# Splitting the first MLP weights differently between two loads, and adding a partial sum one chunk later, in a decode block on one core

## The chip, the cores and the metric

The kernel runs on one core of a Trainium2 chip. The metric is the time on the device of one execution, in microseconds (us); lower is better. Five engines of the core work side by side, each through its own queue of instructions: TensorE (PE, with its weight loads shown as PEld), VectorE (DVE), ScalarE (ACT), GpSimd (POOL) and SyncE (SP), which issues nearly all transfers.

## What is computed

The reference is a transformer block for one new token in each of four sequences: attention over a cache, then an MLP.

```python
B, Sq, D = 4, 1, 448          # attention: 16 query heads, 8 cached heads of 256
W = 1024                      # the last 1024 of 4096 cached positions
q = (layernorm(x) @ wq).reshape(B, Sq, 16, 256)
scores = einsum("bhqd,bhkd->bhqk", q, k) * 256 ** -0.5
o = einsum("bhqk,bhkd->bhqd", softmax(scores), v)
h = x + o.reshape(B, Sq, 4096) @ wo

y = layernorm(layernorm(h))   # the block's layernorm and the MLP's own
u = gelu(y @ w1 + b1)         # w1: 448 x 1792
h2 = h + u @ w2 + b2          # w2: 1792 x 448
```

All arrays are float32.

## The kernel before

The work goes head by head over the eight cached heads. Keys, values and projection weights are laid out on the host so that they come in large transfers, each into a slot of a ring of three (`t0`, `ta`, `tb`, `tc`, `td`, and at the end `te0` to `te2`). The order of TensorE's, SyncE's and ScalarE's instructions is the order of the source; VectorE's and GpSimd's is chosen when the kernel is built. All loads are issued by SyncE on one queue and land one behind the other. The last three slots take, in this order: the last head's keys (`te0`), the values and output weights of head 6 (`te1`), the values of head 7 in three pieces (`te2`), its output weights, then w1 in two pieces (`te0`), and w2 in four pieces of 8, 3, 2 and 1 chunks of 448 columns (`te2`).

The change is in the MLP at the end. There a small number of rows (four sequences) meets large weights, so the output columns are split into four quadrants, which stand on the partitions 0 to 31, 32 to 63, 64 to 95 and 96 to 127. `FQ` is 448, a quarter of the 1792 hidden columns.

- **Statistics.** `h` is the sum behind the attention. `d` and `z` are `h` with its mean taken off, once and twice. ScalarE squares both and sums along the row (`dv`, `zv`). `row_mean` (line 390) folds the four quadrants' sums into one by a matmul with the matrix `fold`. `rsqrt` (lines 145 and 146) adds the epsilon on VectorE and raises to the power of -1/2 on GpSimd. `r1` and then `s`, a product of both roots, come of it.
- **First product.** `z` is transposed to `zT`, in four chunks of 128 features; the last chunk has 64. For each chunk `a`, four matmuls (`j`, one for each quadrant of the hidden columns) add to `pu` (line 429). The weights come from `w1t`, a list of four column ranges of the slot `te0`: three of 1792 columns, and a small one of 896 columns, into whose two halves of the partitions the last 64 features are packed. `w1_part` picks the rows and columns for `a` and `j`. Since the scale `s` belongs to the row, it is applied behind the product: line 442 computes `pu * s + b1` in two column ranges, line 443 the GELU, lines 448 and 450 transpose, and lines 452 and 455 write `gT`.
- **Second product.** The hidden features are 14 chunks (`NFC`). Chunks 0 to 7 go into `pa`, each chunk with one matmul of 448 columns into one of four quadrants (line 462); ScalarE copies `pa` to `pas` (line 466). Chunks 8 to 13 go into `py` with four matmuls each (line 472), one for each quadrant of the output columns. `add_quadrants` (line 253) adds the four quadrants of `pas` into `py` with the matrix `sel`. Line 478 adds `h` and the bias and line 479 writes the output.

`keep_warm` puts matmuls on zeros into waits. A float32 matmul of the source shows as two in the profile, so a chunk of four matmuls is eight in it.

Of the kernel before, what the change touches and what calls it, by code (L numbers as in the profile page):

```python
# [11 lines left out]
ALU = mybir.AluOpType  # L12
# [7 lines left out]
F = 1792  # L20
P = 128
H = P // 2
ND = 4
NKC = W // P
NFC = F // P
FQ = F // 4
Q = 32
CACHE = NKC * B * DH
# [7 lines left out]
def block_kernel(ctx: ExitStack, tc, rows, wq0, k0, wq1, la, lb, lc, ld, k7, vo, w1, w2, out):  # L36
    nc = tc.nc
# [12 lines left out]
    def slot(name):  # L50
        return ring.tile([P, SLOT], F32, tag="r", name=name)

    def load(t, at, src, pieces=None):
        dst = t[:, at : at + src.shape[-1]]
        at = 0
        for n in pieces or (src.shape[-1],):
            nc.sync.dma_start(dst[:, at : at + n], src[:, at : at + n])  # L57
            at += n
        return dst

    def cut(t, sizes):
        parts, at = [], 0
        for n in sizes:
            parts.append(t[:, at : at + n])
            at += n
        return parts
# [18 lines left out]
    def output_weights(t):  # L85
        return t.rearrange("p (j e) -> p j e", j=4)
# [18 lines left out]
    zT = const.tile([P, ND, Q], F32, name="zT")  # L105
# [37 lines left out]
    def rsqrt(dst, var, name):  # L143
        ve = work.tile(list(dst.shape), F32, tag="ve", name=f"ve_{name}")
        nc.vector.tensor_scalar_add(ve, var, EPS)  # L145
        nc.gpsimd.tensor_tensor(dst, ve, mhalf[: dst.shape[0], : dst.shape[1]], op=ALU.pow)  # L146
# [78 lines left out]
    def columns(t, j):  # L225
        if j < 3:
            return t[:, j * P : (j + 1) * P].rearrange("p (i c) -> p i c", i=2)
        return t[:, None, 3 * P :].to_broadcast([t.shape[0], 2, H])
# [22 lines left out]
    def add_quadrants(dst, t, start):  # L251
        for j in range(4):
            nc.tensor.matmul(dst[j * Q : (j + 1) * Q], sel, columns(t, j), start=start, stop=False)
# [76 lines left out]
    e = [slot(f"te{i}") for i in range(3)]  # L330
# [2 lines left out]
    vt, wot = chunks(v), output_weights(wot)  # L333
    vt_last = chunks(load(e[2], 0, vo[1][:, :CACHE], (CACHE // 4, CACHE // 2, CACHE // 4)))
    wo_last = output_weights(load(e[1], CACHE + WEIGHTS, vo[1][:, CACHE:]))
    w1t = cut(load(e[0], CACHE, w1, (2 * F, F + F // 2)), (F, F, F, F // 2))
    w2t = cut(load(e[2], CACHE, w2, (8 * D, 3 * D, 2 * D, D)), NFC * (D,))
    p, rec_last = softmax(g + 1, scores(g + 1, kt))

# [34 lines left out]
    for i in range(4):  # L374
        for j in range(4):
            nc.tensor.matmul(
                ph[j * Q : (j + 1) * Q], oT[(g + 1) % 2][:, i, :], columns(wo_last[:, i, :], j),
                start=False, stop=(i == 3),
# [2 lines left out]

    def w1_part(a, j):
        if a < 3:
            return slice(0, P), w1t[a][:, FQ * j : FQ * (j + 1)]
        rows = slice(H * (j // 2), H * (j // 2) + H)
        return rows, w1t[a][rows, FQ * (j % 2) : FQ * (j % 2 + 1)]


    def row_mean(sums, at, name):
        nc.tensor.matmul(at, fold, sums, start=True, stop=True)  # L390
        return at

    def stat(name):
        return once.tile([P, 1], F32, tag=name, name=name)
# [3 lines left out]
    hs, ds, dv, zv = (stat(n) for n in ("hs", "ds", "dv", "zv"))  # L398
    nc.vector.scalar_tensor_tensor(h, last, 1.0, xb, op0=ALU.mult, op1=ALU.add, accum_out=hs)
    pm = ps_m.tile([P, 2], F32, tag="m", name="pm")  # L400
    m = row_mean(hs, pm[:, 0:1], "m")
# [4 lines left out]
    m = row_mean(ds, pm2[:, 0:1], "m2")  # L406
# [13 lines left out]
    r1 = stat("r1")  # L420
    s = stat("r2")
    u = once.tile([P, FQ], F32, tag="u", name="u")
    pu = ps_s.tile([P, 512], F32, tag="s", name="pu")[:, :FQ]
    pv = ps_m.tile([P, 2], F32, tag="m", name="pv")
    for a in range(ND):
        m = Q if a == 0 else B
        for j in range(4):
            rows, w = w1_part(a, j)
            nc.tensor.matmul(
                pu[j * Q : j * Q + m, :], zT[rows, a, :m], w, start=(a == 0), stop=(a == ND - 1),  # L430
            )
        if a == 0:
            rsqrt(r1, row_mean(dv, pv[:, 0:1], "v1"), "r1")
        if a == 1:
            v2 = stat("v2")
            nc.vector.tensor_scalar(v2, row_mean(zv, pv[:, 1:2], "v2"), r1, r1, op0=ALU.mult, op1=ALU.mult)
            rsqrt(s, v2, "r2")
            nc.vector.tensor_mul(s, s, r1)


    for cols in (slice(0, 2 * P), slice(2 * P, FQ)):
# [16 lines left out]
    first = 8  # L458
    pa = ps_w.tile([P, D], F32, tag="acc", name="pa")
    for c in range(first):  # L460
        j, m = c % 4, Q if c < 4 else B
# [6 lines left out]
    for c in range(first, NFC):  # L468
        for j in range(4):
            m, n = (Q, 2) if c == first else (B, 2 if j < 3 else 1)  # L470
            w = columns(w2t[c], j) if n == 2 else w2t[c][:, None, 3 * P :]
            nc.tensor.matmul(  # L472
                py[j * Q : j * Q + m, :n, :], gT[:, c, :m], w, start=(c == first), stop=(c == NFC - 1),
            )
        if c == first + 1:
            add_quadrants(py, pas, False)
    res = once.tile([P, P], F32, tag="res", name="res")
    nc.vector.tensor_add(res, py.rearrange("p i c -> p (i c)"), hb)
# [72 lines left out]
```

## Time and profile before

| | |
|---|---|
| median of three runs | 214.09 us (214.06 to 214.11) |
| the profiled execution's own time | 214.17 us |
| its span, first to last instruction | 212.4 us |
| TensorE's mean granted clock | 0.847 of full speed |
| busy share of the span: PE, DVE, ACT, POOL | 65%, 18%, 10%, 3% |
| moved by transfers | 88.46 MB, mean 417 GB/s |

The profile is of one execution. The busy share of an engine is that over the whole span; the end of the kernel, where the change lies, has to be read from the timeline and from the chain of work that ended last. In rows of instructions the first number is the start in us from the span's start, the second the duration; `out<-in` names the tiles; square brackets hold the idle time ahead of the instruction and what ended it.

### The profile page before, as it was taken

The page shows a single profiled execution, that of the slowest core. Times are in us where ns is not written, and L with a number is a line of the kernel's source. Part 1 is how long each engine was busy: PE and PEld are TensorE (multiplying, and loading weights), DVE is VectorE, ACT ScalarE, POOL GpSimd, SP SyncE. Part 2 cuts the span into 40 slices and gives each one's busy share as a digit, 9 for nine tenths or more (in the row PEclk, how much of TensorE's full clock was granted, in tenths as well). Part 3 has the DMA queues.
Part 4 walks back from the last instruction along what each step waited for, and adds up shares of the span by engine and source line. Part 5 has one row for each costly group of instructions (what it writes and reads, how often), then busy time and mean ns, then how long its engine had stood idle before and what let it go on. Part 6 is the DMA issues. An engine that isn't in the chain of part 4 may idle for free.

```text
span 212.4 us, 2289 instructions
## 1 busy us (share of the span) xinstructions
PE 138.0 (65%) x965; PEld 47.7 (22%) x965; DVE 38.4 (18%) x167; ACT 21.2 (10%) x52; POOL 5.6 (3%) x17
## 2 busy tenths in 40 slices
PE   0457825862970595189398189238908879997884
PEld 0322211220220221023123022113202322323332
DVE  1420220320230012012214013100301223123220
ACT  2010210110020100012003001101000301010311
POOL 6100000000000000000000000000000000000100
PEclk9999995797698579769859959955965899999999
DMA  7999898989999999989999999998989989999991
GB/s 284 440 388 534 361 488 371 470 374 509 408 395 517 407 407 396 479 382 477 385 477 446 422 407 481 419 442 383 490 349 466 441 384 428 426 407 427 430 400 66
DMA packets 3457, 88.46 MB, mean 417 GB/s; under 512 B 412, under 2 KB 692, under 8 KB 1272
## 3 DMA queue, kind: packets, MB, share of 16 engines
q1 hardware_dynamic: 3392, 88.29, 97.0%
q8 instruction: 7, 0.11, 0.2%
q10 hardware_dynamic: 56, 0.05, 0.1%
q14 instruction: 2, 0.02, 0.0%
HBM read 88.26 MB, written 0.07 MB: 416 GB/s over the span
## 4 chain that ended last, share of the span: by engine, by line
DMA 77%; PE 17%; SPq 2%; DVE 1%; ACT 1%; issue 1%; ACTq 0%
DMA tb<-lb 23%; DMA ta<-la 21%; DMA td<-ld 20%; DMA te<-w 13%; PE s L172 7%; PE po L216 4%; SPq L57 2%; PE pq L152 1%; PE ppt L204 1%; PE acc L245 1%; PE pa L462 1%; SPq L265 1%; PE pqt L158 1%; ACT qs L154 1%; PE py L472 0%
## 5 line engine op out<-in xcount | busy, mean ns | idle before, releaser
L177 DVE TENSOR_REDUCE mx<-s 128x1 f32<-128x512 f32 x16 | 11.1, 691 | 60.5 <-PE s L172 60.5
L172 PE MATMUL s<-ta,qT 128*32 128x512 f32 x64 | 12.7, 966 | 8.1 <-DMA ta<-la 8.1
L154 ACT COPY qs<-pq 128x512 f32<-128x512 f32 x8 | 4.7, 586 | 116.9 <-PE pq L152 116.9
L188 ACT ACTIVATE p<-s,nm 128x512 f32<-128x512 f32 x16 | 10.9, 687 | 46.2 <-DVE nm L184 46.2
L172 PE MATMUL s<-td,qT 128*32 128x512 f32 x32 | 7.3, 1061 | 12.2 <-DMA td<-ld 12.2
L233 DVE TENSOR_SCALAR o<-po,rec 128x512 f32<-128x512 f32 x8 | 6.0, 751 | 46.3 <-PE po L216 46.3
L216 PE MATMUL po<-tb,pT 128*32 128x512 f32 x32 | 7.3, 1061 | 10.6 <-DMA tb<-lb 10.6
L152 PE MATMUL pq<-tc,yT 128*32 128x512 f32 (+1 forms) x20 | 3.9, 891 | 14.7 <-DMA tc<-lc 14.7
L204 PE MATMUL ppt<-ident,p 128*128 128x128 f32 x64 | 10.5, 286 | 0.7 <-ACT p L188 0.4
L216 PE MATMUL po<-tc,pT 128*32 128x512 f32 x64 | 10.6, 823 | 0.0
L158 PE MATMUL pqt<-ident,qs 128*128 128x128 f32 x32 | 6.6, 341 | 6.0 <-ACT qs L154 6.0
L172 PE MATMUL s<-tb,qT 128*32 128x512 f32 x64 | 9.2, 724 | 0.0
L204 PEld LDWEIGHTS ppt<-ident,p 128*128 128x128 f32 x64 | 6.7, 140 | 6.3 <-ACT p L188 6.3
L160 DVE TENSOR_REDUCE sm<-pqt 128x16 f32<-128x64 f32 x8 | 1.8, 224 | 33.7 <-PE pqt L158 33.7
L216 PE MATMUL po<-te,pT 128*32 128x512 f32 x64 | 7.5, 597 | 0.4 <-DMA te<-vo 0.3
L172 PE MATMUL s<-t,qT 128*32 128x512 f32 x32 | 6.2, 953 | 1.9 <-DMA t<-k 1.9
L216 PE MATMUL po<-td,pT 128*32 128x512 f32 x64 | 7.3, 595 | 0.0
L158 PEld LDWEIGHTS pqt<-ident,qs 128*128 128x128 f32 x32 | 4.2, 169 | 12.0 <-ACT qs L154 10.3
L172 PEld LDWEIGHTS s<-ta,qT 128*32 128x32 f32 x64 | 3.0, 168 | 16.8 <-issue 13.9
L237 PE MATMUL pot<-ident,o 128*128 128x128 f32 x32 | 5.3, 287 | 2.2 <-DVE o L233 2.2
L146 POOL TENSOR_TENSOR r<-ve_r,mhalf 128x1 f32<-128x1 f32 x2 | 1.1, 542 | 190.7 <-DVE ve_r L145 190.7
L208 DVE COPY pT<-ppt 128x16 f32<-128x16 f32 x32 | 4.7, 171 | 7.6 <-PE ppt L204 7.6
(131 smaller groups left out, 114.2 us busy)
## 6 DMA issues: line engine op xcount, KB each, us to landing
tc<-lc SPq DMA_DIRECT2D x2, 7936.0 KB
td<-ld SPq DMA_DIRECT2D x2, 7936.0 KB
ta<-la SPq DMA_DIRECT2D x2, 7040.0 KB
tb<-lb SPq DMA_DIRECT2D x2, 7040.0 KB
te<-vo SPq DMA_DIRECT2D x1, 4992.0 KB
t<-k SPq DMA_DIRECT2D x1, 4864.0 KB
te<-k SPq DMA_DIRECT2D x1, 4096.0 KB
te<-w SPq DMA_DIRECT2D x2, 1792.0 KB
```

What stands on the lines that cost most here:

```text
L57: nc.sync.dma_start(dst[:, at : at + n], src[:, at : at + n])
L152: nc.tensor.matmul(pq[j * Q : (j + 1) * Q, cols], y, w, start=True, stop=True)
L154: nc.scalar.copy(qs, pq)
L158: nc.tensor.transpose(pt[:, i, :], qs[:, i * P : (i + 1) * P], ident)
L172: nc.tensor.matmul(s[b * Q : (b + 1) * Q, :], qT[g % 2][:, c, b, :], kt[:, c, b, :], start=(c == 0), stop=(c == 1),)
L177: nc.vector.reduce_max(m, s, axis=AX.X)
L188: nc.scalar.activation(p[:, h * 512 : (h + 1) * 512], halves[h], AF.Exp, bias=nm, scale=SCALE, accum_out=sums[:, h : h + 1],)
L204: nc.tensor.transpose(pt[:, c, :], p[:, (4 * h + c) * P : (4 * h + c + 1) * P], ident)
L208: nc.vector.tensor_copy(pT[g % 2][:, 2 * h : 2 * h + 2, :, i * REP : (i + 1) * REP], src[:, :, i, :, :REP])
L216: nc.tensor.matmul(po[b * Q : (b + 1) * Q], pT[g % 2][:, c, b, :], vt[c][:, :, b, :], start=(c == 0), stop=(c == NKC // 2 - 1),)
L233: nc.vector.tensor_scalar_mul(o, po, rec)
L237: nc.tensor.transpose(pt[:, i, c], o[:, i, c * P : (c + 1) * P], ident)
```

## The change

w1 is still loaded in two pieces, but the pieces are cut at another place. Before, the first held chunks 0 and 1 and the second chunk 2 and the small chunk. Now the small chunk stands behind chunk 1 in the slot and in the host's array, so that the first piece holds chunks 0, 1 and the small one, and the second only chunk 2. The products are made in that order (0, 1, small, 2). The two folds of the statistics and the work on `r1` and `s` behind them stand ahead of all four chunks; before, they stood behind chunk 0 and chunk 1. In the second product, `pas` is added behind chunk 10 in place of chunk 9.

```diff
-    w1t = cut(load(e[0], CACHE, w1, (2 * F, F + F // 2)), (F, F, F, F // 2))
+    w1t = cut(load(e[0], CACHE, w1, (2 * F + F // 2, F)), (F, F, F // 2, F))
...
         if a < 3:
-            return slice(0, P), w1t[a][:, FQ * j : FQ * (j + 1)]
+            return slice(0, P), w1t[3 if a == 2 else a][:, FQ * j : FQ * (j + 1)]
         rows = slice(H * (j // 2), H * (j // 2) + H)
-        return rows, w1t[a][rows, FQ * (j % 2) : FQ * (j % 2 + 1)]
+        return rows, w1t[2][rows, FQ * (j % 2) : FQ * (j % 2 + 1)]
...
-    for a in range(ND):
+    rsqrt(r1, row_mean(dv, pv[:, 0:1], "v1"), "r1")
+    v2 = stat("v2")
+    nc.vector.tensor_scalar(v2, row_mean(zv, pv[:, 1:2], "v2"), r1, r1, op0=ALU.mult, op1=ALU.mult)
+    rsqrt(s, v2, "r2")
+    nc.vector.tensor_mul(s, s, r1)
+    for a in (0, 1, 3, 2):
         m = Q if a == 0 else B
         for j in range(4):
             rows, w = w1_part(a, j)
             nc.tensor.matmul(
-                pu[j * Q : j * Q + m, :], zT[rows, a, :m], w, start=(a == 0), stop=(a == ND - 1),
+                pu[j * Q : j * Q + m, :], zT[rows, a, :m], w, start=(a == 0), stop=(a == 2),
             )
-        if a == 0:
-            rsqrt(r1, row_mean(dv, pv[:, 0:1], "v1"), "r1")
-        if a == 1:
-            v2 = stat("v2")
-            nc.vector.tensor_scalar(v2, row_mean(zv, pv[:, 1:2], "v2"), r1, r1, op0=ALU.mult, op1=ALU.mult)
-            rsqrt(s, v2, "r2")
-            nc.vector.tensor_mul(s, s, r1)
...
-        if c == first + 1:
+        if c == first + 2:
             add_quadrants(py, pas, False)
...
     w1 = packed(np.asarray(B_w1))
+    w1 = np.concatenate([w1[:, : 2 * F], w1[:, 3 * F :], w1[:, 2 * F : 3 * F]], axis=1)
```

## The prediction

> **What bounds the kernel now.** I read the page first, for where the time goes as a whole.
>
> ```profile
> span 212.4 us, 2289 instructions
> ...
> DMA 77%; PE 17%; SPq 2%; DVE 1%; ACT 1%; issue 1%; ACTq 0%
> ```
>
> The chain that ended last is three quarters transfer. The change touches only the last eleven microseconds, so the share says little; what counts is which wait ends last there. Next, therefore, the end of that chain in order of time (start, length, what it was).
>
> ```profile
> 177.69 28.09 DMA te<-w
> 205.78 0.14 issue
> 205.92 1.75 PE pa L462 x16
> ...
> 207.74 0.54 ACT pas L466
> ...
> 209.69 0.29 DVE res L478
> ```
>
> The chain does not pass through the first MLP product, its scaling or the GELU at all. It runs through one transfer into a `te` slot, landed at 205.78 (the 8·D piece of w2, since the partial product `pa` is released by it), then `pa`, the copy `pas`, the last products and the output. So there are two places to judge: does anything ahead of 205.78 matter, and what can be gained behind it. The third view is the timeline, engine by engine, for the stretch ahead of 205.78. Columns: start, duration, engine, line, operation.
>
> ```profile
> 198.10 0.39 PE L345 MATMUL warm<-idle 128*32 128x512 bf16 x1
> 198.44 0.96 PE L429 MATMUL pu<-te,zT 128*32 128x448 f32 x8
> 199.33 0.38 PE L390 MATMUL pv<-dv,fold 128*128 128x1 f32 x2
> 199.64 0.93 PE L429 MATMUL pu<-te,zT 128*4 128x448 f32 x8
> 200.50 0.38 PE L390 MATMUL pv<-zv,fold 128*128 128x1 f32 x2
> 201.31 1.80 PE L429 MATMUL pu<-te,zT 128*4 128x448 f32 x16 [0.42 <-DMA te<-w]
> ```
>
> ```profile
> 199.75 0.16 DVE L145 TENSOR_SCALAR ve_r<-pv 128x1 f32<-128x1 f32 x1 [1.36 <-PE pv L390]
> 201.00 0.28 DVE L436 TENSOR_SCALAR v<-pv,r 128x1 f32<-128x1 f32 x1 [1.09 <-PE pv L390]
> 201.31 0.15 DVE L145 TENSOR_SCALAR ve_r<-v 128x1 f32<-128x1 f32 x1
> 202.12 0.16 DVE L438 TENSOR_TENSOR r<-r,r 128x1 f32<-128x1 f32 x1 [0.66 <-POOL r L146]
> 203.25 0.81 DVE L442 SCALAR_TENSOR_TENSOR u<-pu,r,rs 128x256 f32<-128x256 f32 x2 [0.97 <-PE pu L429]
> 205.35 0.21 DVE L452 COPY gT<-put 128x48 f32<-128x48 f32 x1 [1.29 <-PE put L450]
> ```
>
> The 16 matmuls from 201.31 are chunks 2 and 3 of the first MLP product, released by the second load of w1. They end at 201.31 + 1.80 = 203.11, DVE's scaling follows at 203.25, and `gT` is written at 205.35 + 0.21 = 205.56. `pa` could have gone then; its weights landed 0.22 us later. The chain of the first product thus has 0.22 us to spare.
>
> **The change, part 1: w1's split and its order.** Removed: TensorE's wait of 0.42 us ahead of 201.31, for everything but chunk 2. Added: 448 KB in the first load, and that load's landing is now later. The size of the second load, and when the two landings let TensorE go, stand in the issues and in the instructions of lines 429 and 390:
>
> ```profile
> te<-w SPq DMA_DIRECT2D x1, 1344.0 KB
> ```
>
> ```profile
> L429 PEldq EVENT_SEMAPHORE  x1: 51/51/51, 198.0 to 198.0; - x1
> ```
>
> ```profile
> L390 PEldq EVENT_SEMAPHORE  x1: 51/51/51, 199.9 to 199.9; - x1
> ```
>
> The first load let TensorE go at 198.0, the second at 201.31. In these 3.3 us 1344 KB landed, so 448 KB more in the first take 3.3 / 3 = 1.1 us: it lands at 199.1, and the second, behind the same bytes in the same queue, still at 201.3. Nothing is added to the queue in bytes, transfers or order, so the w2 pieces stay at their times, 205.78 among them.
>
> With the products held to 199.1, the two sums go first. The fold of `dv` can follow the warm matmul: 198.10 + 0.39 = 198.49. Its reader on DVE starts 0.42 after it (199.33 to 199.75) and takes 0.16, to 199.07. The fold of `zv` writes the same small tile: in the row above its semaphore wait stands at 199.9, when that DVE reader is done (199.75 + 0.16), so it now starts at 199.1. A product follows a fold by 0.31 (199.33 to 199.64): the first is at 199.42, and the load of 199.1 is no wait. Queued behind this new wait for DVE on TensorE are all sixteen product groups; this 0.3 us is counted in the 199.42.
>
> Four chunks then run without a break: 0.96 for the first, and for each further one at most 1.80 - 0.93 = 0.87, which is what the second of two chunks added at 201.31 with its change from whole to half rows. The end is 199.42 + 0.96 + 3 x 0.87 = 202.99, against 203.11: 0.12 us earlier. If the wait for DVE costs nothing, 0.3 us more. Chunk 2, now last, starts at 202.99 - 0.93 = 202.06, behind its load's 201.31, so no wait takes the old one's place. The scale `s` was ready at 202.12 + 0.16 = 202.28, 1.78 after its fold at 200.50; it comes at 199.1 + 1.78 = 200.9, two microseconds before DVE needs it.
>
> So `gT` is ready at 205.1 to 205.45 instead of 205.56. The cover over this gain is the landing at 205.78, and it is complete: part 1 is worth **0 us**. Both ends: up to 0.14 gained (the step "issue" ahead of `pa`, if some of it is `gT` and not the transfer); a loss only if the chain slips by 0.12 + 0.22 = 0.34 us against my sum. I take 0, as the chain's own row names the transfer.
>
> **Part 2: `pas` folded in behind chunk 10.** Here nothing is hidden by w2's first piece.
>
> ```profile
> 207.42 0.64 PE L472 MATMUL py<-te,gT 128*32 128x128 f32 x16
> 208.32 0.43 PE L253 MATMUL py<-pas,sel 128*32 128x128 f32 x8 [0.27 <-ACT pas L466]
> 208.57 1.05 PE L472 MATMUL py<-te,gT 128*4 128x128 f32 x32
> ```
>
> Chunks 8 and 9 are the 16 matmuls at 207.42. TensorE is then idle until `pas` is copied (207.74 + 0.54 = 208.28), and the eight matmuls with `sel` start at 208.32. Chunks 10 to 13 are the last 32, in 1.05. The length of one is in the group's row (ns: least, median, most):
>
> ```profile
> L472 PE MATMUL py<-te,gT x48: 219/272/273, 207.4 to 209.3; 128*4 128x128 f32 x30, 128*4 128x64 f32 x10, 128*32 128x128 f32 x8
> ```
>
> The last one's 0.27 is its way through the array, so one chunk takes (1.05 - 0.27) / 4 = 0.20 to issue. Chunk 10 is in the same piece of w2 as 8 and 9, so it needs nothing new, and its 0.20 goes into the idle 0.27. Put ahead of `sel`, it delays `sel` by nothing: 207.42 + 0.64 + 0.20 = 208.26, before 208.28. If that cover were gone (`pas` ready earlier), chunk 10 would cost its 0.20 there again, and the sum would be zero.
>
> Behind `sel` there are then three chunks, 0.20 us less. What is late next is w2's last piece, needed by chunk 13 alone. Its landing stands in no row; the two stretches around its end bound it:
>
> ```profile
> 208.20:208.40 0.20, 0.08 (x4) 0.08 (x8) 0.00 (x0) 0.07 (x1) 0.00 (x0) 1.00 0.35 134
> 208.40:208.60 0.20, 0.20 (x12) 0.20 (x16) 0.00 (x0) 0.00 (x0) 0.00 (x0) 1.00 0.01 0
> ```
>
> The last columns are the busy share of the transfer engines and GB/s: the stream's last bytes move at about 208.4. Chunk 13 started at 208.57 + 3 x 0.20 = 209.17, in one run with the others, so its weights were there; it now can at 208.57 + 2 x 0.20 = 208.97. The landing lies between 208.4 and 209.17: at the early end the gain is 0.20 us, at the late end 0. I take **0.15 us**, nearer the early end, since from 208.4 on nothing moves and 208.97 is 0.5 us behind that.
>
> The sum: 0 + 0.15. The profiled execution took 214.17 us (span 212.4 and 1.8 around it), so 214.02; it stands 0.08 above the median of 214.09, which gives **213.94 us**. A measurement of this kernel can tell about 0.2%, 0.43 us, from no change, so I forecast no difference. The forecast's own range is 213.75 to 214.10.
>
> **The rivals.** The rate of the stream by stretches:
>
> ```profile
> 190.00:195.00 5.00, 4.05 (x47) 1.59 (x43) 1.10 (x3) 0.00 (x0) 0.00 (x0) 1.00 1.05 443
> 201.00:204.00 3.00, 2.55 (x19) 0.42 (x19) 1.34 (x5) 0.24 (x1) 0.54 (x1) 1.00 0.98 410
> 204.00:206.00 2.00, 1.47 (x15) 1.15 (x19) 0.26 (x2) 0.77 (x4) 0.00 (x0) 1.00 0.95 387
> 206.00:208.00 2.00, 2.00 (x32) 0.76 (x31) 0.00 (x0) 0.26 (x1) 0.00 (x0) 1.00 0.82 322
> ```
>
> *Faster: w2 lands sooner.* The stream ran at 443 GB/s in 190 to 195, but at 410 and 387 in 201 to 206. If that was TensorE's work beside it, and the new order takes it away, the 3 x 410 + 2 x 387 = 2004 KB would pass in 4.5 us instead of 5: 0.48 gained at 205.78, 0.63 in all, **213.46**. It decides from about 0.28 us on; part 1's lead is then needed, and its 0.11 to 0.45 with the 0.22 to spare gives it. Against it: bytes, order and number of transfers are the same, and the transfer engines are 95 to 98% busy as it is. Chance 0.16.
>
> *Slower: the smaller second load runs worse.* Its 896 KB (1344 - 448) take 2.2 us at the pace of the 3.3 us for 1344. At the 322 GB/s of the last of these rows they would take 2.85, so 0.65 later at 205.78, 0.50 in all with the 0.15 gained: **214.59**. It decides at about 330 GB/s, below which the loss passes 0.43. For it there is only that row, in which the queue runs empty; against it the first, in which the value pieces ahead of w1 were moving:
>
> ```profile
> te<-vo SPq DMA_DIRECT2D x1, 896.0 KB
> ```
>
> A piece of the very size was in that part of the queue, and the stretch stands at 443. Chance 0.07. The Trainium skill has a rule that speaks for this rival (DMA: Bandwidth & Descriptors, section Measured): transfers should be at least 1 MiB to reach 75% of peak, with 341 GB/s stated for 1 MB; by its figure the second load would take an estimated 2.7 us, and the total would be near 214.5. The 443 GB/s with an 896 KB piece in the queue disagrees, since here transfers queue behind each other.
>
> *Slower: TensorE's clock falls.* `gT` is ready earlier but `pa` is not, so TensorE rests up to 0.8 us before 205.92. If that halved its clock, `pa` up to chunk 8 (205.92 to 207.42, 1.5 us) and what follows `sel` (208.32 to 209.35, 1.0 us) would double: **216.4**. Against it: the clock column stands at 1.00 in all these rows, and still in the one without any matmul:
>
> ```profile
> 210.00:212.00 2.00, 0.00 (x0) 0.00 (x0) 0.00 (x0) 0.00 (x0) 0.00 (x0) 1.00 0.11 33
> ```
>
> Chance 0.03. The Trainium skill (TensorE: Matmul & The Clock Gate, What's actually happening) puts the fall behind an idle window of some 3.4 us; the 2 us without a fall agree.
>
> *The change doesn't do what it says*: chunk 10 does not fit ahead of `pas`, or chunk 13 waits as long as before; 214.09. Chance 0.05.
>
> **How the numbers follow.** The forecast has the rest, 0.69. With the last rival, 0.74 are within 0.2%; faster by more 0.16; slower by more 0.07 + 0.03 = 0.10. The range goes from 213.50 (half of the faster rival) to 214.25 (the forecast's end, and the smaller part of a slower load), and leaves out about 0.18.
>
> **What would show it.** Right: line 390's four matmuls ahead of line 429's first, at about 198.5 and 199.1; line 429 from about 199.4 without a wait for a transfer, ended near 203.0; `pa` at 205.9 all the same, released by the transfer; 24 matmuls of line 472 ahead of `sel` at 208.3, 24 behind it, and `res` at 209.5 to 209.6. Wrong: `pa` off 205.9 by over 0.2 in either direction, which says that the stream's timing moved; a wait for chunk 2's load; a clock below 1.00 behind 198; or `sel` later than 208.4.

## The result, and the profile after

The changed kernel took **215.06 us** in the median of 22 executions, the kernel before 214.06 in the median of 22; the ratio is 1.0030, interval 1.0017 to 1.0043. It is slower by 0.3%, a small difference, but one that the interval tells from no change; the forecast of 213.94 (213.50 to 214.25) was wrong. But the median stands for no typical execution: ten took 213.80 to 214.11 (median 213.94), ten 215.04 to 215.39, two 216.45 and 216.50. The kernel before has nothing of the kind: 213.90 to 214.42. Below, an execution over 214.7 us is called long.

The profile after was taken from a short one (214.09 us, span 212.3). TensorE from the statistics to the end, start and duration first:

```profile
198.31 0.39 PE L345 MATMUL warm<-idle 128*32 128x512 bf16 x1
198.63 0.38 PE L390 MATMUL pv<-dv,fold 128*128 128x1 f32 x2
199.35 0.35 PE L390 MATMUL pv<-zv,fold 128*128 128x1 f32 x2 [0.34 <-DVE ve_r L145]
199.64 3.44 PE L434 MATMUL pu<-te,zT 128*32 128x448 f32 x32
...
205.91 1.71 PE L460 MATMUL pa<-te,gT 128*32 128x448 f32 x16 [0.33 <-DMA te<-w]
207.49 0.86 PE L470 MATMUL py<-te,gT 128*32 128x128 f32 x24
208.32 0.43 PE L253 MATMUL py<-pas,sel 128*32 128x128 f32 x8
208.56 0.95 PE L470 MATMUL py<-te,gT 128*4 128x128 f32 x24
```

```profile
209.11 0.11 PEld L470 LDWEIGHTS py<-te,gT 128*4 128x4 f32 x8 [0.23 <-DMA te<-w]
```

```profile
205.31 0.21 DVE L450 COPY gT<-put 128x48 f32<-128x48 f32 x1 [1.29 <-PE put L448]
209.58 0.29 DVE L476 TENSOR_TENSOR res<-py,hb 128x128 f32<-128x128 f32 x1 [4.06 <-PE py L470]
```

This is the order of the forecast, line by line: the sums first, products without a wait to 203.08 (forecast 202.99), `gT` ready at 205.52, `pa` at 205.91 behind w2 all the same, `sel` at 208.32, `res` at 209.58, 0.11 earlier than before. Only chunk 13, whose weight loads stand at 209.11, waits for w2's last piece. That the short executions' median is the forecast to the hundredth is in part luck: against 214.06 it is 0.12 lower, not 0.15, and in the next set of executions the short ones stood at 214.03. What the profile does not show is why half of the executions are a microsecond longer.

### The profile page after: what moved, and what is told of

It reads as the page before. It is cut to its first block, busy times and chain, and to the rows that moved or that the text cites. A ratio compares the mean times of both kernels' runs of the same rounds, so it can differ in the third digit from the quotient of the medians.

```text
span 212.3 us, 2288 instructions
## 1 busy us (share of the span) xinstructions
PE 133.5 (63%) x965; PEld 47.0 (22%) x965; DVE 38.4 (18%) x167; ACT 21.2 (10%) x52; POOL 5.6 (3%) x17
## 4 chain that ended last, share of the span: by engine, by line
DMA 77%; PE 17%; SPq 2%; DVE 1%; issue 1%; ACT 1%; ACTq 0%
DMA tb<-lb 23%; DMA ta<-la 21%; DMA td<-ld 20%; DMA te<-w 14%; PE s L172 7%; PE po L216 4%; SPq L57 2%; PE ppt L204 1%; PE acc L245 1%; PE pq L152 1%; PE pa L460 1%; PE py L470 1%; SPq L265 1%; PE pqt L158 1%; ACT qs L154 1%
## 5 line engine op out<-in xcount | busy, mean ns | idle before, releaser
L172 PE MATMUL s<-ta,qT 128*32 128x512 f32 x64 | 11.5, 882 | 9.5 <-DMA ta<-la 9.5
L172 PE MATMUL s<-tb,qT 128*32 128x512 f32 x64 | 8.2, 657 | 0.0
L172 PE MATMUL s<-t,qT 128*32 128x512 f32 x32 | 5.0, 779 | 1.9 <-DMA t<-k 1.9
```

Of the source, the lines that this page charges most:

```text
L172: nc.tensor.matmul(s[b * Q : (b + 1) * Q, :], qT[g % 2][:, c, b, :], kt[:, c, b, :], start=(c == 0), stop=(c == 1),)
```

## The experiments

**First four: the long execution itself, and the change in parts.** The theories: (A) TensorE's clock falls, (B) transfers land later, (C) instructions or tables are fetched late.

The changed kernel again (no edit):

> The changed kernel again, to get a profile of one of its long executions (12 of 22 stood at 215.0 to 216.5, the rest at 213.8 to 214.1). Theory A, TensorE's clock: a long execution shows a granted clock of 0.5 somewhere behind 196, and transfers that land at the same times as in the short one (first w2 piece at about 205.8). Theory B, the transfers: the clock stays at 1.00, and w1's or w2's pieces land 1.2 us later or more. Theory C, instructions or tables fetched late: an engine stands still with clock and landings unchanged. Times 213.8 to 214.1 and 215.0 to 216.5 again, about half each.

5 of 12 were long, and the profiled one was (215.09). Busy time by stretch; the columns are PE, PEld, DVE, ACT and POOL, then the granted clock, the share of the transfer engines and GB/s:

```profile
196.88:200.30 3.42, 2.88 (x23) 1.69 (x26) 1.17 (x7) 2.09 (x5) 0.60 (x2) 1.00 1.02 429
200.30:203.71 3.41, 3.41 (x24) 0.29 (x20) 0.16 (x1) 0.00 (x0) 0.49 (x1) 0.50 0.97 405
203.71:207.12 3.41, 2.87 (x26) 1.42 (x22) 1.02 (x3) 0.82 (x3) 0.00 (x0) 1.00 0.97 390
```

```profile
199.47 5.02 PE L434 MATMUL pu<-te,zT 128*32 128x448 f32 x32
...
207.06 1.71 PE L460 MATMUL pa<-te,gT 128*32 128x448 f32 x16
```

The clock is at 0.50 for 3.41 us in the midst of the first product, which takes 5.02 instead of 3.44. `pa` starts at 207.06, now held by `gT` and no more by w2, and the chain that ended last runs through the GELU:

```profile
205.63 0.84 PE put L446 x6
206.47 0.22 PE put L448 x4
206.70 0.32 PE warm L345
207.02 0.04 issue
207.06 1.75 PE pa L460 x16
...
210.61 0.29 DVE res L476
```

w2's transfer is no longer in the chain, the stream moves 405 and 390 GB/s (385 in the kernel before between 202.7 and 206.1), and its last bytes move between 208.2 and 208.4, as in the kernel before, so B falls; in the stretch at half clock TensorE is busy for all of its 3.41 us, so it lacks no instructions, and C falls. A it is: the product is longer because it runs at half clock. Of the 1.58 us that the product lost, 1.03 arrive at the end (210.61 against 209.58); the rest went into the cover ahead of `pa` and an earlier start.

Part 1 alone:

```diff
-        if c == first + 2:
+        if c == first + 1:
             add_quadrants(py, pas, False)
```

> The new cut of w1, the new order of the chunks and the sums ahead; the partial sum added behind chunk 9 as before. Theory A: the long executions stay, 215 to 216.5 in about half; the short ones at 214.0 to 214.2, without the tail's 0.1. Theory B: the same. If the tail's new place made them, all executions are at 214.0 to 214.2.

8 of 12 were long (median of the short 213.95); ratio 1.0044, interval 1.0021 to 1.0067. The tail's new place is not needed for it.

Part 2 alone, the kernel before with the inverse of these lines:

> The kernel before with only the partial sum added behind chunk 10. Theories A and B alike: no long executions, 213.8 to 214.1, 0.1 to 0.15 us under the kernel before. If the tail made the long ones, they are here.

None of 11 was long; median 213.95, ratio 0.9993 (0.9985 to 1.0002). The tail of its profile:

```profile
205.87 1.71 PE L462 MATMUL pa<-te,gT 128*32 128x448 f32 x16
207.44 0.86 PE L472 MATMUL py<-te,gT 128*32 128x128 f32 x24
208.28 0.42 PE L253 MATMUL py<-pas,sel 128*32 128x128 f32 x8
208.53 0.95 PE L472 MATMUL py<-te,gT 128*4 128x128 f32 x24
```

The 24 matmuls ahead of `sel` have filled TensorE's idle 0.27, as forecast.

The split and order of chunks alone, with the sums at their old places:

```diff
-    w1t = cut(load(e[0], CACHE, w1, (2 * F, F + F // 2)), (F, F, F, F // 2))
+    w1t = cut(load(e[0], CACHE, w1, (2 * F + F // 2, F)), (F, F, F // 2, F))
...
-    for a in range(ND):
+    for a in (0, 1, 3, 2):
```

> The new cut of w1 and the new order of its chunks (0, 1, small, 2), with the two sums at their old places behind the first and the second chunk product, and the partial sum behind chunk 9. The first product then starts at about 199.1 to 199.2, when the first load lands, instead of 198.44. Theory A (too little work on TensorE for too long ahead of the first product, 195.9 to 199.6 in the changed kernel): fewer long executions than with the sums ahead, or none, as the light stretch is half a us shorter. Theory B (the larger first load): as many as with the sums ahead.

7 of 12 were long and longer (215.8 to 217.2), and even the short ones stood at 214.25 to 214.49: the first product waits for the load and the sums still interrupt it. My expectation under A, fewer long ones than with the sums ahead, missed. The profiled execution took 217.18:

```profile
196.21:199.63 3.42, 2.50 (x17) 1.30 (x17) 1.04 (x5) 1.89 (x5) 0.00 (x0) 1.00 0.99 417
199.63:203.04 3.41, 3.41 (x20) 1.07 (x12) 0.16 (x1) 0.20 (x1) 0.54 (x1) 0.50 1.04 438
203.04:206.45 3.41, 3.41 (x18) 0.56 (x19) 0.59 (x3) 0.00 (x0) 0.54 (x1) 0.50 0.95 386
```

```profile
199.19 1.34 PE L429 MATMUL pu<-te,zT 128*32 128x448 f32 x8 [0.72 <-DMA te<-w]
```

Two windows (stretches of 3.41 us between possible changes of the clock) at half clock in a row, so 217.

**What counts as work.** The busy column does not explain the fall: TensorE was busy for 2.88 of 3.42 us ahead of it, while the clock stayed up behind this window of the kernel with less warming (below):

```profile
196.63:200.04 3.41, 2.61 (x19) 1.25 (x23) 0.98 (x5) 2.09 (x5) 0.02 (x1) 1.00 1.01 426
```

In the profile the ends of matmuls are modelled, and one of a single column is shown as busy for about 0.25 us. So I counted streamed columns, the columns of the operand that passes through the array, as a time. A warming matmul of 512 columns in bfloat16 takes 0.21 us in a row of them; four float32 matmuls of 448 columns, which run side by side in the quadrants, take 0.375 (in the kernel before, the groups of four of line 462 start at 205.92, 206.29, 206.67 and 207.04), half the rate for each column. With these two rates each matmul gets a length from its start, doubled at half clock; the share of a window is the part of its 3.41 us that these lengths cover, overlaps counted once.

The windows are placed as the clock's own changes in each trace lie. In the fourteen profiles of this case 455 such windows began at full clock behind 30 us. Behind all 104 with a share up to 0.374 the clock fell; behind all 351 from 0.377 on it did not. With float32 counted at the full rate the two sets would mix: windows up to 0.29 fell, and windows from 0.18 on did not. Where the windows lie differs from execution to execution (their bounds are at 196.88 in the one profile above and at 196.21 in the other). If every placing is as likely, a stretch of work has long executions in proportion to how many placings of a window are under 0.375.

In the kernel before, the least share of any placing behind 191 is 0.416. In the changed one, in the profile of a short execution, it is 0.20, at starts near 196.0, and placings over 1.66 us (starts from 195.4 to 197.05) are under the bound: 1.66 / 3.41 = 0.49 of the executions. The half clock that follows such a window begins at 198.8 to 200.5, on or just ahead of the first product. Long were 12 of 22 and 5 of 12.

**The second four: fill the stretch, empty it elsewhere, split part 1.** When I wrote their expectations I counted float32 at the full rate, hence the lower shares in them.

Three more warming matmuls:

```diff
-    keep_warm(1, warm)
+    keep_warm(2, warm)
     h = once.tile([P, P], F32, tag="h", name="h")
...
     m = row_mean(hs, pm[:, 0:1], "m")
-    keep_warm(1, warm)
+    keep_warm(2, warm)
...
     rsqrt(r1, row_mean(dv, pv[:, 0:1], "v1"), "r1")
+    keep_warm(1, warm)
     v2 = stat("v2")
```

> The changed kernel with three more warming matmuls of 512 columns (0.21 us each on TensorE): one ahead of h, one behind the fold of hs, one between the folds of dv and zv, each in a wait that TensorE has there anyway. Theory A (TensorE's clock is halved for a window of 3.41 us when the window before held too few streamed columns; the least share over all placings of a window is 0.30 of the time in the kernel before and 0.19 in the changed one, at window starts of 195.5 to 197): the least share is back at about 0.3, so all executions are at 213.8 to 214.2. If the long executions have another cause, about half stay at 215 and more.

2 of 12 were long, where none was expected; the others took 213.84 to 213.99. One of the two was profiled (215.23), and the fall is in another place:

```profile
203.27:206.68 3.41, 2.45 (x24) 1.49 (x27) 0.69 (x3) 1.01 (x4) 0.00 (x0) 1.00 0.96 390
206.68:210.10 3.42, 3.42 (x58) 2.38 (x50) 0.00 (x0) 0.53 (x1) 0.00 (x0) 0.50 0.28 110
```

```profile
205.78 2.38 PE L461 MATMUL pa<-te,gT 128*32 128x448 f32 x16 [0.46 <-DMA te<-w]
```

This is the stretch behind the first product, where `gT` is early and TensorE rests for w2: share 0.36, and `pa` and all behind it at half clock. It is the rival of the prediction in the place where the prediction had it. The added matmuls do not touch this stretch. In the profile of the changed kernel's short execution its least share is 0.40, and in the kernel before 0.42, close above the bound, so a few tenths of a us between the first product and w2's landing can decide here.

The kernel before, with less warming:

```diff
     m = row_mean(hs, pm[:, 0:1], "m")
-    keep_warm(1, warm)
...
     m = row_mean(ds, pm2[:, 0:1], "m2")
-    keep_warm(1, warm)
```

> The kernel before, with the warming matmul behind the fold of hs and the one behind the fold of ds left out (two of 0.21 us), and nothing else changed: same loads, same order of sums and products. Theory A: the least share of a window falls from 0.30 to about 0.2, so long executions appear, some by one us or more. If the cut of w1 or the order of the sums makes the long ones in any other way, all are at 213.9 to 214.3.

9 of 12 were long, with every load, sum and product of the kernel before in its place. So neither the cut nor the order is needed for long executions, only too few columns. Which window fell in each of the nine is not known. In the profiled one (215.72) it was one behind the first product, in an execution whose w2 came 0.3 us late (`pa` at 206.21):

```profile
203.45:206.87 3.42, 2.50 (x22) 1.35 (x23) 0.86 (x3) 1.01 (x4) 0.00 (x0) 1.00 0.95 381
206.87:210.28 3.41, 3.41 (x45) 1.83 (x41) 0.00 (x0) 0.53 (x1) 0.00 (x0) 0.50 0.27 104
```

That stretch holds the same work as in the kernel before, so this one execution says nothing of the two matmuls left out; the count, 9 of 12 against 1 of 134, does.

The sums ahead, with w1 cut as before:

```diff
+    rsqrt(r1, row_mean(dv, pv[:, 0:1], "v1"), "r1")
...
     for a in range(ND):
...
-        if a == 0:
-            rsqrt(r1, row_mean(dv, pv[:, 0:1], "v1"), "r1")
```

> The kernel before with only the two sums ahead of the four products; w1 cut and ordered as before, partial sum behind chunk 9. The second fold waits for VectorE's reading of the first, so the first product starts near 199.5 to 199.6 although its weights are there at 198.0. Theory A: the light stretch is as long as in the changed kernel, and long executions come in about half of the runs. If the larger first load makes them, there are none.

8 of 10 were long; ratio 1.0051 (1.0030 to 1.0071). The profile of one:

```profile
199.13 0.35 PE L390 MATMUL pv<-zv,fold 128*128 128x1 f32 x2 [0.34 <-DVE ve_r L145]
199.42 4.96 PE L434 MATMUL pu<-te,zT 128*32 128x448 f32 x32
```

No wait for a transfer stands ahead of it, and the first product still starts a microsecond later than in the kernel before, behind the two folds and the wait for VectorE between them. Each half of part 1 alone, the cut with its order or the sums ahead, empties the stretch.

One more warming matmul only (the last of the three lines above):

> The changed kernel with one more warming matmul, between the folds of dv and zv, where TensorE waits 0.3 us for VectorE. Theory A: the least share rises from 0.19 to about 0.25, so long executions stay but are rarer, at window starts of 195.5 to 196.3 only: some 1 to 4 of 12 rather than half.

5 of 12 were long, more than the 1 to 4 expected; by the count of columns at the half rate for float32, 1.24 us of placings stay under the bound, 0.36 of the executions.

**The third three: fill both stretches.** Six more warming matmuls, the three above and:

```diff
-    keep_warm(3, warm)
+    keep_warm(4, warm)
     put = ps_m.tile([P, 4, 4, B], F32, tag="m", name="put")
...
-    keep_warm(1, warm)
+    keep_warm(3, warm)
 
     first = 8
```

> The changed kernel with the three warming matmuls ahead of the first product and three more in the second light stretch, between the first product and pa (one ahead of the transposes of u, two ahead of pa), where the profile with three shows the clock fall at 206.7 after TensorE had waited for w2. Theory A: the least share of streamed columns in any window of 3.41 us behind 191 is then above 0.3, so no execution is longer than 214.3; median 213.9, that is 0.1 to 0.2 under the kernel before. If long executions stay in a sixth or more, another cause is at work.

1 of 11 was long (215.43), where none was expected, and the median of 214.04 is not 0.1 to 0.2 under the kernel before (214.05 beside it) but level with it. Placings over 0.40 us around 196.3 are still under the bound, at 0.32 at the least.

The kernel before with part 2 and the same warming matmuls, without the one between the folds:

> The kernel before with the partial sum behind chunk 10 and the same extra warming matmuls except that between the folds; w1's cut and the sums as before. If the new cut and order of w1 are worth nothing, as predicted, since pa waits for w2's first piece, this stands within 0.05 us of the changed kernel with six warming matmuls: 213.9. If they are worth their lead on gT (0.2 to 0.3 us), it stands that much above it.

None of 11 was long; median 214.09, against 214.01 for the short ones of the changed kernel with six. The 0.08 between them is more than the 0.05 expected and less than the 0.2 to 0.3 of the other case, with the single executions spread over 0.26 and 0.50: part 1 is worth nothing that can be told here. Neither kernel came to the 213.9 expected, so part 2's 0.1 does not show in the times beside the warming matmuls.

Only the second stretch filled (the lines of this group's diff, without the three above):

> The changed kernel with only the three warming matmuls of the second stretch. Theory A: the first stretch (window starts of 195.5 to 197, least share 0.19) is as before, so 4 to 7 of 12 executions are long, at 215 to 216.6. If the second stretch alone made the long ones, there are none.

6 of 12 were long, 215.25 to 215.43, as expected: the first stretch makes them. In the profiled one (215.39) the half clock stands from 199.79 to 203.21, over the first product.

**The last: eight.** One more behind the fold of `ds` and one behind the transposes of `z`:

> The changed kernel with eight more warming matmuls: the six before, one more behind the fold of ds and one more behind the transposes of z. By the traces so far, the clock falls behind a window of 3.41 us in which columns stream for less than about 0.375 of the time (float32 counted at the half rate that its spacing shows): with six, windows that start within 0.4 us around 196.3 are still under it (share 0.33), which makes 0.4 / 3.41 = 0.12 of the executions long; 1 of 11 was. Theory A: with eight the least share is above 0.38 and no execution is over 214.4; median 213.9 to 214.1. The two may cost up to 0.1 us each on the way to gT, which pa's wait for w2 covers. If long ones stay at one in ten, the rule is wrong or something else is left.

None of 11 was long (213.96 to 214.19, median 214.06; ratio 0.9999, 0.9990 to 1.0008). The least share is 0.447. By the count alone 11 executions cannot tell none from one in ten; the least share is the stronger sign. The four windows of its profile, as the clock's changes place them:

```profile
195.50:198.91 3.41, 3.40 (x27) 1.56 (x20) 1.42 (x7) 1.10 (x5) 0.00 (x0) 1.00 0.97 409
198.91:202.33 3.42, 3.40 (x33) 1.08 (x37) 0.75 (x4) 0.99 (x1) 1.09 (x2) 1.00 1.06 445
202.33:205.74 3.41, 3.13 (x28) 1.61 (x25) 1.02 (x3) 0.71 (x3) 0.00 (x0) 1.00 0.94 387
205.74:209.15 3.41, 3.34 (x72) 2.00 (x72) 0.00 (x0) 0.82 (x3) 0.00 (x0) 1.00 0.57 223
```

All kernels together; the share expected is the width of the placings under 0.375 over 3.41. It was worked out afterwards, from the one profile of each kernel, with the bound read off these same profiles. For the kernel with three warming matmuls most of its 0.40 is the second stretch of the long execution that was profiled; the first stretch alone would give 0.11.

| kernel | expected | long | median of the short |
|---|---|---|---|
| before (all its runs) | 0 | 1 of 134 | 214.05 to 214.10 |
| part 2 alone | 0 | 0 of 11 | 213.95 |
| part 2 and five warming | 0 | 0 of 11 | 214.09 |
| changed, eight warming | 0 | 0 of 11 | 214.06 |
| changed, six | 0.12 | 1 of 11 | 214.01 |
| changed, one | 0.36 | 5 of 12 | 213.90 |
| changed, three | 0.40 | 2 of 12 | 213.91 |
| changed | 0.49 | 17 of 34 | 213.94 and 214.03 |
| part 1 alone | 0.49 | 8 of 12 | 213.95 |
| sums alone | 0.49 | 8 of 10 | 214.09 |
| changed, second stretch filled | 0.53 | 6 of 12 | 213.94 |
| before, two warming left out | 0.67 or more | 9 of 12 | 213.97 |
| split alone | 0.71 | 7 of 12 | 214.34 |

None of these is a version that can be told from the kernel before as faster; part 2 alone comes nearest, at 0.9993 with an interval that reaches 1.0002.

## Why the prediction was wrong

- **Part 1, worth 0**: right for the executions in which the clock holds. `pa` stayed at 205.91, released by w2, with `gT` ready at 205.52; filled with warming matmuls, the kernel with part 1 and that without it stand within 0.08 us. The terms: where the products wait for the first load, in the split alone, it let TensorE go at 199.19 (199.1 forecast); in the changed kernel they began at 199.64 (199.42), in a profile in which the warming matmul ahead already stood 0.21 later (198.31 against 198.10), and took 3.44 (3.57 at most).
- **Part 2, 0.15**: right in kind; 0.11 in the profiles after and 0.14 in that of part 2 alone (`res` at 209.58 and 209.55 against 209.69). The working took the landing of w2's last piece to be near 208.4, as nothing moves from there on. But chunk 13's weight loads were let go at 209.11, near the late end of the bound (the stream moves its last bytes between 208.4 and 208.6, at 27 GB/s), and in this profile the wait takes about half of the 0.20.
- **The rival "TensorE's clock falls", 0.03**: this step failed, in three ways. First, it looked at the rest ahead of `pa` only. The step that moved the first product from 198.44 to 199.42 was in the same text, and it was given a cost of time but none for the clock. What it took out of the stretch ahead of 199.2 was chunk 0's two rounds of four matmuls, 0.75 us of streaming, and with them the least share of a window there went from 0.42 to 0.20, under the 0.375 at which the clock holds. Second, the row of 210 to 212, without matmuls at clock 1.00, was taken to show that a rest of that length is harmless; a stretch of 2 us cannot show it, since in these traces the clock follows the share of a whole window of 3.41 us. Third, the price: 216.4 came of half clock on `pa` and behind it; in the profiled long execution the half clock hit the first product instead, for 1.03 us at the end, 215.09, and ten of the twelve long ones stand at 215.0 to 215.4.
- Beside it the prediction set the rule of the Trainium skill (TensorE: Matmul & The Clock Gate, What's actually happening), a fall behind an idle window of some 3.4 us. The length agrees, 3.41 at half clock in the profile of the long execution. The word idle does not: the window from 196.88 to 200.30, behind which the clock fell, had a share of 0.373.
- **The rivals of the transfers**: neither happened. In the short execution `pa` was released at the same time as before, 205.91 against 205.92, so w2 landed neither sooner nor later behind the smaller second load.

What stays open: the executions of 216.5 in the changed kernel were not caught in a profile. Two windows at half clock in a row would make them, as in the profile of the split alone, and so might a second fall on `pa`; neither is shown. The one long execution of the kernel before (215.87) was not caught either. Its second stretch would have a share of 0.33 if `pa` came 0.3 us later, as in the profile with less warming; that is an estimate from the count, and it would make the execution long.

## What to carry to other kernels

A step moved later takes its work away from where it was, and in this kernel that work on TensorE was also what kept the clock up: list, beside the waits, how many columns stream in every stretch as long as a clock window, at every placing of it. Warming matmuls have to be set for the stretch as it is after the change, and a change that empties a stretch shows in some executions only, so one profile can look better while the median is worse. Busy time is no measure of it; streamed columns are.

## What was not expected of the hardware

In the fourteen profiles of this case the clock is halved behind a window in which columns streamed for less than about 0.375 of the time: behind 104 windows up to 0.374 it fell, behind 351 from 0.377 on it stayed, with float32 counted at half the rate of bfloat16. It came back behind windows at half clock with a share of 0.77 and more (117 of them) and not behind those with 0.74 and less (150). The split alone, whose products are interrupted by the folds, had 0.54 in its first window at half clock, and so stayed at half clock for a second.
